# A block difference in expert 0's output: taken from the weights instead of from the result

## The chip, the cores and the metric

The kernel runs on one core of a Trainium2 chip. The metric is the device time of one execution in microseconds; the time before is the median of 13 executions, 684.53 us (684.03 to 687.27). The engines are TensorE (PE in the profile; PEld is its weight load), VectorE (DVE), ScalarE (ACT), GpSimd (POOL) and SyncE (SP), which here only issues DMAs. Each engine works through its own instruction list in the order in which it was written down; semaphores make one engine wait for another.

## The reference

Two layers follow each other. An attention with a narrow band and block summaries takes q, k, v of 4 batches, 8 heads, 768 positions and 64 features, and gives x, 3072 tokens by 512 features. Then a mixture of 8 experts works on x:

```python
logits = x @ w_gate
logits = logits - logits.max()
P = np.exp(logits)
for _ in range(8):                      # Sinkhorn: rows, then columns
    P /= P.sum(1, keepdims=True) + 1e-09
    P /= P.sum(0, keepdims=True) + 1e-09
    P *= N / E
out = np.zeros((N, D), dtype=np.float32)
for e in range(E):
    h = np.maximum(x @ w1[e], 0.0)      # 3072 x 1024
    ye = h @ w2[e]                      # 3072 x 512
    out += P[:, e:e + 1] * ye
```

Every token passes through every expert, so the two matrix products of eight experts are most of the work.

## The kernel before

**Attention and expert 0 (up to about 175 us of the trace).** The attention goes by pairs of heads, four pairs to a batch. Expert 0 is computed beside it in the plain way, because it can begin as soon as a batch's x is there: tokens go in halves of a batch (384 tokens, function `expert0`, called with `t0` = 0, 384, ... 2688). A half has eight hidden blocks (`hidden0`, matmuls at L199, relu on ACT or DVE) and three output tiles of 128 tokens (`project0`, matmuls at L204 that read `w2s[0]`); a tile goes to `out_acc[:, t, :]` with a copy (L195). In `out_acc` it stands unscaled, since the weights P are not known yet.

The order of this stage is not written out by hand. `add(...)` gives a planner (`Plan`) units of work with an engine, a cost in microseconds, the units that they depend on and a priority; the planner simulates the engines and issues the units in the order that comes out. Units of expert 0's matmuls have low priority (1000 and up) and fill gaps; their evacuations have -1.0, which goes ahead of the attention's own units (0 to 35). PSUM tiles are rings of a few buffers ("m" has three, "a" three, "s" one). After the attention, `bridge` adds the Sinkhorn rounds (DVE, POOL and PE in turn) and the first groups of expert 1 to the same plan, and the rest of expert 0's matmuls fill in between.

**Experts 1 to 7 (from about 175 us on).** Here both products are done by a seven-product (Strassen-Winograd) scheme on blocks of halves: tokens t and t + 1536 are taken together. The hand-written loop over `n` computes in each round one hidden group (`group`: four 128-row weight blocks times 512 token pairs, products `p1` to `p7`) and one output pair (`pair`: tile `ta` of the first 1536 tokens and tile `tb` of the second, products `q1` to `q7`). A round has the order `q1 p1 ... q5 v5 ... p6 c2 ... p2 r11 q6 v6 p3 c12 p7 c22 r12 q2 q4 q3 r22 s1 s3 p4 s2 q7`, with names in `p` and `q` on PE, `r12 r22 s1 s2 s3 s4 c12 c22 v5 ya yb` on DVE and the rest on ACT. Into DVE's list between `s4` and `c12` some rounds put sums of weights or of x for the next expert (`w2_sum`, `w1_sums`, `x_sum`). The lines to know: L817 writes `hf<-pb,c` (`c12`), `hf<-pg,c` (`c22`) and `xy<-xy,c` (`v5`); L928 is `r12`, L931 is `r22`, both a relu in place on 128x512 fp16; L1010 is `ya`/`yb`.

The seven-product scheme gives for tile `tb` not the two column halves of the output but the second half and the difference second minus first. So `out_acc[:, tb, 0:DH]` holds, through experts 1 to 7, the difference; `fin` turns it back after expert 7. What expert 0 left there has to be brought into that form. This is done in `scale0`, once for each of the 12 pairs of expert 1, at the end of rounds n = 4 to 15: ACT multiplies both tiles by P[:, 0] (L965), and then GpSimd (L967) replaces the first half columns by second minus first.

POOL's list holds, besides, the loads of the next expert's weights (L175 for w1, L186 for w2), which it issues as DMAs.

Of the kernel before, what the change touches and what calls it, by code (L numbers as in the profile page):

```python
# [13 lines left out]
ALU = mybir.AluOpType  # L14
# [19 lines left out]
class Plan:  # L34
# [12 lines left out]
    def add(self, eng, cost, fn, deps=(), prio=0.0, opens=(), uses=(), lag=0.0):  # L47
        u = Unit(eng, cost, fn, [d for d in deps if d is not None], prio, list(opens), lag)
        for b in list(opens) + list(uses):
            b.users.append(u)  # L50
        if uses and eng != "PE":
            u.prio -= 100.0
        self.waiting.append(u)
        return u
# [62 lines left out]
def kernel(  # L117
# [10 lines left out]
    nc = tc.nc  # L128

    B, H, S, D = q.shape  # L130
    G = S // 128
    N, DM = out.shape
# [3 lines left out]
    KF = F // 128  # L136
# [8 lines left out]
    HG = G // 2  # L145
# [19 lines left out]
    out_acc = persist.tile([128, NT, DM], FP32)  # L165
# [3 lines left out]
    w1s, w2s = {}, {}  # L169
# [27 lines left out]
    def hidden_mm(e, hp, t0, n, f):  # L197
        for dk in range(KD):
            nc.tensor.matmul(hp[:, 0:n], lhsT=w1s[e][:, dk, 128 * f:128 * (f + 1)],  # L199
                             rhs=xT[:, dk, t0:t0 + n], start=(dk == 0), stop=(dk == KD - 1))  # L200

    def project_mm(e, yp, h, c, fs):
        for f in fs:
# [17 lines left out]
    if True:  # L221
# [16 lines left out]
        add = plan.add  # L238
# [291 lines left out]
        def project0(key, c, part):  # L530
            if part == 0:
                at["yp", key, c] = bank("m", "yps")
            project_mm(0, at["yp", key, c], at["h", key], c, range(4 * part, 4 * part + 4))
# [62 lines left out]
        U = {}  # L596
# [114 lines left out]
        def expert0(t0, xs):  # L711
            key, n = t0, len(halves)
            halves.append(key)
            pr = 1000.0 + n
            w = [U["w1", i] for i in range(2)]
            evac, old = [], [U.get(("pj", halves[n - 2], c)) for c in range(HG)] if n >= 2 else []
            for f in range(KF):
                buf = Buffer("m")

                def fn(f=f):  # L720
                    at["hp", key, f] = hidden0(key, t0, f)
                m = U["hd", key, f] = add("PE", 0.67, fn, xs + [w[f // 4]] + old, pr + f * 0.01, opens=[buf])

                def ev(f=f):
                    relu(U["rl", key, f].on, at["h", key][:, f, 0:HS], at.pop(("hp", key, f))[:, 0:HS])
                U["rl", key, f] = add({"ACT": 0.5, "DVE": 0.56}, 0, ev, [m], -1.0, uses=[buf])
                evac.append(U["rl", key, f])
                zero.extend([m, evac[-1]])
            for c in range(HG):
                buf = Buffer("m")  # L730
                p0 = add("PE", 0.88, lambda c=c: project0(key, c, 0), evac[0:4] + [U["w2"]],
                         pr + 0.1 + c * 0.02, opens=[buf])
                p1 = add("PE", 0.88, lambda c=c: project0(key, c, 1), evac[4:8] + [p0],
                         pr + 0.11 + c * 0.02, uses=[buf])
                U["pj", key, c] = p1

                def ev(c=c):
                    copy(U["yo", key, c].on, out_acc[:, t0 // 128 + c, :], at.pop(("yp", key, c))[:])
                U["yo", key, c] = add({"ACT": 0.58, "DVE": 0.68}, 0, ev, [p1], -1.0, uses=[buf])
                zero.extend([p0, p1, U["yo", key, c]])  # L740

        def gate(b, xs, prio):
            buf = Buffer("a")
            U["lg", b] = add("PE", 0.65, lambda: logits(b), xs, prio, opens=[buf])
            U["lo", b] = add("ACT", 0.25, lambda: logits_out(b), [U["lg", b]], prio, uses=[buf])
# [27 lines left out]
        for i in range(PB, NP):  # L773
            load_pair(i)
            pair_start(i, 20 + i)
            pair_whole(i, 20 + i)
            if i % PB == PB - 1:
                b = i // PB
                xs = [U["x", PB * b + d] for d in range(PB)]
                gate(b, xs, 900 if b < B - 1 else 0)  # L780
                expert0(b * S, xs)
                expert0(b * S + HS, xs)
        for i in range(4):
# [15 lines left out]
    if True:  # L799
# [148 lines left out]
        def pair(e, j, c, spare=False, c1_at=None):  # L948
            def h(q):
                return lambda f: hs[e, j, f][:, q, :]  # L950
            ta, tb = 4 * j + c, HT + 4 * j + c
            B = {}

            def part(*ks):
                if not spare:
                    return B["x"][:, ks[0]:ks[-1] + 1:max(1, ks[-1] - ks[0]), :]
                t, k = B["xy"[ks[0] // 2]], ks[0] % 2
                return t[:].rearrange("p (k d) -> p k d", k=2)[:, k:k + 1, :]

            def at(k):  # L960
                return part(k)[:, 0, :]

            def scale0():
                for t in (ta, tb):
                    nc.scalar.activation(out=out_acc[:, t, :], in_=out_acc[:, t, :], func=AF.Copy,  # L965
                                         scale=P_sb[:, t, 0:1])
                nc.gpsimd.tensor_tensor(out=out_acc[:, tb, 0:DH], in0=out_acc[:, tb, DH:DM],  # L967
                                        in1=out_acc[:, tb, 0:DH], op=ALU.subtract)

            def q1():  # L970
                if spare:
                    B["x"] = fps.tile([128, 512], FP32, tag="ab", name="px", bufs=2)
                    B["y"] = fps.tile([128, 512], FP32, tag="g", name="py", bufs=2)
                else:
                    B["x"] = xps.tile([128, 4, DH], FP32, tag="xy", name="xy", bufs=2)
                product2(e, c, at(0), h(A11), "B11", True)

            def c1():
                B["c1"] = c1_at if c1_at is not None else fast.tile([128, DH], FP32, tag="c1", name="c1", bufs=1)[:]
                nc.scalar.copy(out=B["c1"], in_=at(0))  # L980

            def q5():
                product2(e, c, at(1), h(S1), "T1", False)

            def v5():
                plus(at(2), at(1), B["c1"])

            def q6():
                product2(e, c, at(2), h(S2), "T2", False)

            def v6():
                nc.scalar.copy(out=at(3), in_=at(2))

            def q2():
                product2(e, c, at(0), h(A12), "B21", False)

            def q7():
                product2(e, c, at(2), h(S3), "T3", False)

            def q3():  # L1000
                product2(e, c, at(3), h(S4), "B22", False)

            def q4():
                product2(e, c, at(1), h(A22), "T4", False)

            def add(t, k, *src):
                src = part(*src)
                w = src.shape[1]
                acc = out_acc[:, t, k * DH:(k + w) * DH].rearrange("p (h d) -> p h d", h=w)
                nc.vector.scalar_tensor_tensor(out=acc, in0=src, scalar=P_sb[:, t, e:e + 1], in1=acc,  # L1010
                                               op0=ALU.mult, op1=ALU.add)

            def store(t, k=slice(0, DM)):
                nc.sync.dma_start(out=out[t * 128:(t + 1) * 128, k], in_=out_acc[:, t, k])

            def ya():
                add(ta, 0, 0, 3)
                if e == E - 1:
                    store(ta)

            def yb():
                add(tb, 0, 1, 2)

            def fin():
                if e == E - 1:
                    sub(out_acc[:, tb, 0:DH], out_acc[:, tb, DH:DM], out_acc[:, tb, 0:DH])
                    store(tb)

            def y_half():
                add(ta, 1, 3)  # L1030
                add(tb, 1, 2)
                store(tb, slice(DH, DM))
                sub(out_acc[:, tb, 0:DH], out_acc[:, tb, 0:DH], out_acc[:, tb, DH:DM])
                nc.vector.tensor_scalar_mul(out=P_sb[:, tb, 0:1], in0=P_sb[:, tb, e:e + 1], scalar1=-1.0)

            def x_half():
                add(ta, 0, 0)
                store(ta)
                nc.vector.scalar_tensor_tensor(
                    out=out_acc[:, tb, 0:DH], in0=at(1), scalar=P_sb[:, tb, 0:1],  # L1040
                    in1=out_acc[:, tb, 0:DH], op0=ALU.mult, op1=ALU.subtract)
                store(tb, slice(0, DH))

            return {f.__name__: f for f in (scale0, q1, c1, q5, v5, q6, v6, q2, q7, q3, q4, ya, yb, fin, y_half, x_half)}
# [204 lines left out]
```

## Time and profile before

The profiled execution took 684.53 us; its span on the core was 682.8 us, the other 1.7 us lie around it.

| | value |
|---|---|
| median of 13 executions | 684.53 us |
| profiled execution, time / span | 684.53 / 682.8 us |
| DVE busy | 589.5 us (86%) |
| ACT busy | 407.3 us (60%) |
| POOL busy | 134.7 us (20%) |
| POOL's subtraction L967 | 12 times, 719 to 832 ns, first at 178.2, last at 248.9 us |
| matmuls of expert 0, L199 and L204 | 256 and 192 |
| granted TensorE clock | 0.999 |

Reading it: busy time is an average over stages. The trace gives every instruction's start and duration, so a stage with a loop can be judged by the time from one round to the next, and the engine that holds it up by who waits for whom. The ends of matmuls are modelled (several in a row overlap in the listing), so on PE starts are compared with starts.

### The profile page before, as it was taken

The page shows a single profiled execution, that of the slowest core. Times are in us where ns is not written, and L with a number is a line of the kernel's source. Part 1 is how long each engine was busy: PE and PEld are TensorE (multiplying, and loading weights), DVE is VectorE, ACT ScalarE, POOL GpSimd, SP SyncE. Part 2 cuts the span into 40 slices and gives each one's busy share as a digit, 9 for nine tenths or more (in the row PEclk, how much of TensorE's full clock was granted, in tenths as well). Part 3 has the DMA queues.
Part 4 walks back from the last instruction along what each step waited for, and adds up shares of the span by engine and source line. Part 5 has one row for each costly group of instructions (what it writes and reads, how often), then busy time and mean ns, then how long its engine had stood idle before and what let it go on. Part 6 is the DMA issues. An engine that isn't in the chain of part 4 may idle for free.

```text
span 682.8 us, 13662 instructions
## 1 busy us (share of the span) xinstructions
PE 669.0 (98%) x5189; PEld 439.0 (64%) x5189; DVE 589.5 (86%) x1444; ACT 407.3 (60%) x785; POOL 134.7 (20%) x177
## 2 busy tenths in 40 slices
PE   8999999899999999999999999999999999999996
PEld 4666666555666666666666666666666666666665
DVE  6878988777799998999789988998899888998886
ACT  4777877555677765555555555555555555555551
POOL 8699810122213120100101010201010101000000
PEclk9999999999999999999999999999999999999999
DMA  9999990000504023310513050404131051301224
GB/s 117 189 145 144 124 115 7 1 1 0 70 9 47 2 31 48 30 18 1 78 17 32 1 78 1 48 1 60 19 31 17 8 71 17 32 1 48 78 93 155
DMA packets 113618, 33.90 MB, mean 50 GB/s; under 512 B 99984, under 2 KB 110736, under 8 KB 113552
## 3 DMA queue, kind: packets, MB, share of 16 engines
q0 software_dynamic: 104672, 26.22, 42.0%
q1 hardware_dynamic: 8352, 6.80, 3.3%
q8 instruction: 40, 0.66, 0.4%
q14 instruction: 26, 0.21, 0.1%
q10 hardware_dynamic: 528, 0.02, 0.0%
HBM read 52.45 MB, written 6.29 MB: 86 GB/s over the span
## 4 chain that ended last, share of the span: by engine, by line
PE 82%; DVE 12%; issue 2%; DMA 1%; POOL 1%; ACT 1%; DVEq 0%; ACTq 0%
PE xy L873 31%; PE pg L867 14%; PE pb L867 9%; PE pa L867 9%; PE yps L204 6%; PE hps L199 6%; DVE hf L817 3%; DVE out_acc L1010 2%; PE tkq L299 1%; PE sg L318 1%; DVE hf L814 1%; DVE hf L928 1%; DVE xy L817 1%; DMA vx<-in_v_dram 1%; PE vs L326 1%
## 5 line engine op out<-in xcount | busy, mean ns | idle before, releaser
L873 PEld LDWEIGHTS <-hf 128*128 128x128 f16 x2352 | 230.0, 98 | 100.3 <-issue 7.0
L873 PE MATMUL xy<-w,hf 128*128 128x256 f16 x1312 | 183.4, 273 | 0.0
L873 PE MATMUL xy<-ws,hf 128*128 128x256 f16 x984 | 147.6, 272 | 2.3 <-DVE xy L817 1.9
L190 ACT ACTIVATE hf<-pg 128x512 f16<-128x512 f32 x84 | 50.2, 597 | 152.8 <-PE pg L867 152.8
L1010 DVE SCALAR_TENSOR_TENSOR out_acc<-xy,P_sb,out_acc 128x512 f32<-128x512 f32 x164 | 115.0, 742 | 1.3 <-PE xy L873 1.3
L814 DVE TENSOR_TENSOR hf<-hf 128x512 f16<-128x512 f16 x252 | 98.9, 420 | 8.5
L867 PE MATMUL pa<-xT,w 128*128 128x512 f16 x336 | 99.9, 379 | 0.0
L867 PEld LDWEIGHTS <-w 128*128 128x128 f16 x672 | 65.7, 98 | 44.5 <-issue 0.5
L817 DVE TENSOR_TENSOR hf<-pb,c 128x512 f16<-128x512 f32 x84 | 57.9, 690 | 35.6 <-PE pb L867 33.9
L175 POOL DMA_DIRECT2D w<-in_moe_w_dram x56 | 41.9, 759 | 185.3 <-PE pg L867 156.9
L867 PEld LDWEIGHTS <-ws 128*128 128x128 f16 x504 | 49.3, 98 | 24.9
L901 ACT COPY c<-pg 128x512 f32<-128x512 f32 x84 | 49.2, 586 | 22.4 <-PE pg L867 22.4
L817 DVE TENSOR_TENSOR hf<-pg,c 128x512 f16<-128x512 f32 x84 | 57.0, 679 | 0.1
L190 ACT ACTIVATE hf<-pa 128x512 f16<-128x512 f32 x84 | 50.6, 602 | 1.1 <-PE pa L867 1.1
L886 ACT COPY pg<-pa 128x512 f32<-128x512 f32 x84 | 47.9, 570 | 4.7
L867 PE MATMUL pg<-xTs,w 128*128 128x512 f16 x168 | 50.0, 379 | 0.2
L867 PE MATMUL pg<-xT,w 128*128 128x512 f16 x168 | 50.0, 379 | 0.0
L867 PE MATMUL pb<-xTs,ws 128*128 128x512 f16 x168 | 50.0, 379 | 0.0
L867 PE MATMUL pb<-xT,ws 128*128 128x512 f16 x168 | 50.0, 379 | 0.0
L867 PE MATMUL pg<-xTs,ws 128*128 128x512 f16 x168 | 50.0, 379 | 0.0
L894 ACT COPY c<-pb 128x512 f32<-128x512 f32 x84 | 49.7, 592 | 0.0
L199 PE MATMUL hps<-xT,w 128*128 128x384 f16 x256 | 48.9, 326 | 0.0
(136 smaller groups left out, 847.9 us busy)
## 6 DMA issues: line engine op xcount, KB each, us to landing
w<-in_moe_w_dram POOLq DMA_DIRECT2D x8, 1024.0 KB, 9.5
w<-in_moe_w_dram POOLq DMA_DIRECT2D x56, 128.0 KB, 3.6
out_dram<-out_acc SPq DMA_DIRECT2D x22, 256.0 KB, 2.0
qst<-in_q_dram POOLq DMA_DIRECT2D x32, 96.0 KB, 5.9
vx<-in_v_dram POOLq DMA_DIRECT2D x16, 192.0 KB, 6.5
kst<-in_k_dram POOLq DMA_DIRECT2D x24, 96.0 KB, 6.1
w<-in_moe_w_dram POOLq DMA_DIRECT2D x2, 512.0 KB, 8.3
kst<-in_k_dram POOLq DMA_DIRECT2D x4, 192.0 KB, 5.2
```

Of the source, the lines that this page charges most:

```text
L175: nc.gpsimd.dma_start(out=t[:, :, h, :], in_=moe_w1[e].rearrange("(dk p) f -> p dk f", p=128)[:, :, f:f + 128])
L190: nc.scalar.activation(out=out, in_=in_, func=AF.Relu, bias=0.0, scale=1.0)
L199: nc.tensor.matmul(hp[:, 0:n], lhsT=w1s[e][:, dk, 128 * f:128 * (f + 1)], rhs=xT[:, dk, t0:t0 + n], start=(dk == 0), stop=(dk == KD - 1))
L204: nc.tensor.matmul(yp[:], lhsT=h[:, f, c * 128:(c + 1) * 128], rhs=w2s[e][:, f, :], start=(f == 0), stop=(f == KF - 1))
L814: nc.vector.tensor_tensor(out=out, in0=in0, in1=in1, op=ALU.subtract)
L817: nc.vector.tensor_tensor(out=out, in0=in0, in1=in1, op=ALU.add)
L867: nc.tensor.matmul(bank[:], lhsT=w[:, dk, :], rhs=x[:, dk, :], start=start and dk == 0, stop=dk == KH - 1, skip_group_check=True)
L873: nc.tensor.matmul(bank, lhsT=a(f)[:, 128 * c:128 * (c + 1)], rhs=w[:, f, :], start=start and f == 0, stop=f == FH - 1, skip_group_check=True)
L886: nc.scalar.copy(out=B["g"][:], in_=B["a"][:])
L894: nc.scalar.copy(out=B["c5"][:], in_=B["b"][:])
L901: nc.scalar.copy(out=B["c2"][:], in_=B["g"][:])
L1010: nc.vector.scalar_tensor_tensor(out=acc, in0=src, scalar=P_sb[:, t, e:e + 1], in1=acc, op0=ALU.mult, op1=ALU.add)
```

## The change

Expert 0's projection for the second 1536 tokens uses, in the first half columns, w2[:, second half] - w2[:, first half], which gives the difference directly: (h @ B) - (h @ A) = h @ (B - A). `w2_difference` writes it over the first half columns of `w2s[0]`, in four DVE instructions of 128x(2x256) fp16. They depend on all twelve output tiles of the first 1536 tokens (which still need the old columns), and every projection of the second 1536 tokens depends on them. They have priority -1.0. The subtraction on GpSimd is taken out of `scale0`.

```diff
+    def w2_difference(f):
+        f = slice(f, f + KF // 4)
+        nc.vector.tensor_tensor(out=w2s[0][:, f, 0:DM // 2], in0=w2s[0][:, f, DM // 2:DM],
+                                in1=w2s[0][:, f, 0:DM // 2], op=ALU.subtract)
...
-                p0 = add("PE", 0.88, lambda c=c: project0(key, c, 0), evac[0:4] + [U["w2"]],
+                p0 = add("PE", 0.88, lambda c=c: project0(key, c, 0), evac[0:4] + (U["w2d"] if t0 >= N // 2 else [U["w2"]]),
                          pr + 0.1 + c * 0.02, opens=[buf])
...
                 gate(b, xs, 900 if b < B - 1 else 0)
+                if b == B // 2:
+                    done = [U["pj", t, c] for t in halves for c in range(HG)]
+                    U["w2d"] = [add("DVE", 0.33, lambda f=f: w2_difference(f), done, -1.0)
+                                for f in range(0, KF, KF // 4)]
+                    zero.extend(U["w2d"])
                 expert0(b * S, xs)
                 expert0(b * S + HS, xs)
...
                     nc.scalar.activation(out=out_acc[:, t, :], in_=out_acc[:, t, :], func=AF.Copy,
                                          scale=P_sb[:, t, 0:1])
-                nc.gpsimd.tensor_tensor(out=out_acc[:, tb, 0:DH], in0=out_acc[:, tb, DH:DM],
-                                        in1=out_acc[:, tb, 0:DH], op=ALU.subtract)
```

## The prediction

> **What bounds the kernel now.** I read the page's busy times first, then the distance from round to round in the listing of PE by time, then one round on all engines, then the stretch of the attention in which the new instructions will stand.
>
> ```profile
> PE 669.0 (98%) x5189; PEld 439.0 (64%) x5189; DVE 589.5 (86%) x1444; ACT 407.3 (60%) x785; POOL 134.7 (20%) x177
> ```
>
> PE is busy for 98% of the span, so a change can only win where PE loses time. The list of who waits for whom puts few waits on PE after 175 us, but busy times and waits are rough here because the ends of matmuls are modelled. The starts of one instruction per round, the product p3, are exact:
>
> ```profile
> 182.75 0.59 PE L867 MATMUL pb<-xT,ws 128*128 128x512 f16 x2
> ...
> 247.00 0.59 PE L867 MATMUL pb<-xT,ws 128*128 128x512 f16 x2
> 253.43 0.59 PE L867 MATMUL pb<-xT,ws 128*128 128x512 f16 x2
> 259.50 0.59 PE L867 MATMUL pb<-xT,ws 128*128 128x512 f16 x2
> ```
>
> From 253.43 to 259.50 is 6.07 us; the rounds from 260.21 to 320.99 (starts of c12 in DVE's listing) take 60.78 / 10 = **6.078** us each, with PE back to back. From 182.75 to 253.43 eleven rounds take 70.68 us, **6.43** each: 0.35 us per round more for the same matmuls. The round before (176.12 to 182.75) took 6.63. These are the twelve rounds with the GpSimd subtraction. One of them, all engines:
>
> ```profile
> 202.73 0.69 DVE L817 TENSOR_TENSOR hf<-pb,c 128x512 f16<-128x512 f32 x1 [0.26 <-PE pb L867]
> 203.34 0.68 DVE L817 TENSOR_TENSOR hf<-pg,c 128x512 f16<-128x512 f32 x1
> ...
> 203.91 0.73 POOL L967 TENSOR_TENSOR out_acc<-out_acc 128x256 f32<-128x256 f32 x1 [5.70 <-ACT out_acc L965]
> 203.94 0.85 DVE L928 TENSOR_SCALAR hf<-hf 128x512 f16<-128x512 f16 x1
> ...
> 204.71 0.28 DVE L931 TENSOR_SCALAR hf<-hf 128x512 f16<-128x512 f16 x1
> ...
> 207.24 0.59 PE L867 MATMUL pa<-xT,w 128*128 128x512 f16 x2
> ...
> 207.55 0.42 DVE L817 TENSOR_TENSOR xy<-xy,c 128x256 f32<-128x256 f32 x1
> ...
> 208.03 0.60 PE L873 MATMUL xy<-ws,hf 128*128 128x256 f16 x4 [0.19 <-DVE xy L817]
> ...
> 209.16 0.69 DVE L817 TENSOR_TENSOR hf<-pb,c 128x512 f16<-128x512 f32 x1 [0.26 <-PE pb L867]
> ```
>
> The columns are start, duration, engine, line, operation; the bracket is idle time before it and who ended it. DVE does c12 and c22, then POOL's subtraction starts at 203.91, and r12, which starts 0.03 us later, takes 0.85 us. Further down, PE begins `pa` at 207.24; two matmuls take it to 207.67 (starts 0.43 apart), but its next product q6 starts at 208.03, 0.06 after v5 ended on DVE (207.55 + 0.42 = 207.97). So 0.36 us of PE is lost to DVE once a round. The same place in a round without POOL:
>
> ```profile
> 297.28 0.68 DVE L817 TENSOR_TENSOR hf<-pg,c 128x512 f16<-128x512 f32 x1
> ...
> 297.88 0.28 DVE L928 TENSOR_SCALAR hf<-hf 128x512 f16<-128x512 f16 x1
> ...
> 298.08 0.28 DVE L931 TENSOR_SCALAR hf<-hf 128x512 f16<-128x512 f16 x1
> ```
>
> There r12 takes 0.28 us. The stage is held by a DVE list made 0.57 us longer (0.85 - 0.28) by POOL; everything after r12 comes later by that.
>
> **The removed subtraction.** Twelve of them, 0.73 us each on POOL, which is 20% busy: their own time is worth nothing. Their worth is what they do to DVE. The chain that closes in a round is c12 to v5 on DVE (202.73 to 207.97, 5.24 us), v5 to q6 to p3 on PE and to the next c12 (207.97 to 209.16, 1.19). Sum 6.43, the measured round. With r12 at 0.28 it is 6.43 - 0.57 = 5.86, below the 6.08 that PE needs. So PE is next, with 0.22 to spare, and a round gains 0.35, not 0.57. DVE's total work does not hold it either: 6.43 less 0.26 idle less 0.57 is 5.60 per round, and 5.86 in the rounds with four 0.28 us weight sums in place of one sum of 0.68. ACT keeps its two scalings (1.34 us); in the round shown it then idled 1.00 us for PE before the next relu, so it is not late.
> Sum over the stage: eleven rounds, 70.68 - 11 x 6.078 = 3.82. The first round gains 0.27: its 6.63 becomes 6.08 + 0.28, because p4 waits there for a c22 that follows four sums of w2, with or without POOL. Together 4.1. Against it: in the round at 228.80, c12 starts 0.29 us after its engine fell free, for no reason that I find in the trace; I let that remain and take off 0.25. **3.85 us.**
>
> In POOL's list the weight loads at 178.87 to 181.31 stood behind the first subtraction at 178.20. They can now go as soon as their buffers are free, up to some 5 us earlier. Expert 2's w2 is first summed at 201.79, so nothing waits for them and no store runs then: 0.
>
> Here the Trainium skill is to be weighed. "SBUF — State Buffer", section "Who interferes with whom", calls the DVE/GpSimd port pair an exclusive lock: the second to come is blocked until the first has finished. By that, r12 would lose 0.70 us (203.94 to 204.64) and the twelve rounds 8.4; by the row it is 0.57, and 6.8. Both exceed PE's 0.35, so the sum is the same by either; that the later instruction pays is what matters.
>
> **The added subtractions.** Four DVE tensor_tensor, 512 fp16 elements per partition each, both inputs in SBUF. The nearest row has the same size and type:
>
> ```profile
> L814 DVE TENSOR_TENSOR hf<-hf x252: 361/418/747, 140.9 to 666.3; 128x512 f16<-128x512 f16 x126
> ```
>
> Median 0.418, so 4 x 0.42 = **1.67** us of DVE. Bounds: 0.38 each where such instructions follow each other (two took 0.76 at 205.55), 0.75 each if they met something on POOL; POOL is idle from 100 to 125 us, so I take 0.42. This stretch of the trace is where the built program puts them:
>
> ```profile
> 109.36 1.04 PE L204 MATMUL yps<-w,h 128*128 128x512 f16 x4
> ...
> 110.20 0.48 DVE L337 COPY Ve<-Ve 64x650 bf16<-64x650 bf16 x1
> ...
> 110.61 0.54 DVE L367 TENSOR_TENSOR em<-er,band 128x768 bf16<-128x768 bf16 x1
> ...
> 112.26 0.55 DVE L367 TENSOR_TENSOR em<-er,band 128x768 bf16<-128x768 bf16 x1
> ```
>
> The twelfth tile of the first half ends with the projection at 109.36 (to 110.40); DVE is free of the copy at 110.68. The instruction order of the changed program has on DVE: two differences, relu, difference, relu, difference, relu, then both mask products `em` (before: 110.61 and 112.26), then the four edge instructions. With the rows' durations and the relus not before their matmuls (the first at 111.78), the last difference ends at 113.75 and the second `em` at 115.4, where it was 112.81; the edges end at 116.3, where it was 114.83. Who waits for that:
>
> ```profile
> 114.85 0.35 PE L390 MATMUL av<-vx,em 128*128 128x65 bf16 x6
> ...
> 119.07 2.75 PE L204 MATMUL yps<-w,h 128*128 128x512 f16 x12
> ```
>
> The attention's values (114.85) need the edges. The planner has put a score product (0.31 us from start to start) and two hidden blocks (0.65 each) ahead of them on PE: work that was to come later anyway, 1.6 us, to 116.5. So 1.6 us of lateness is covered by 1.6 of work. If the cover fails, PE stands for the difference: 0 to 1.5 us. The relus of hidden blocks that wait behind the differences free "m" buffers: that of the third hidden block ends at 114.3, and the PE product that needs its buffer comes at about 115.2. The new wait (projections of the second 1536 tokens for the differences) is met with ease: such a projection first stands on PE at 119.07, in the new order at about 119.3, 5.5 us after 113.75. From the next-but-one projection on PE's order is as before; gate and Sinkhorn begin where they did (DVE idled 3.27 us before the Sinkhorn's first reduction at 126.97). DVE was busy only 2.48 of the 5 us from 120 to 125, where the lateness is worked off. Below zero: a reordered plan can also close one of the small gaps here; PE shows no more than some 0.5 us of them. Bounds -0.4 to +1.5, taken **+0.2**, near the lower end since the cover was worked out row by row.
>
> A rule speaks against the change: "Perfetto Trace Analysis", "Optimizing Scalar/DVE Operations", says that when DVE is saturated, moving work from it to GpSimd may make sense. DVE is 86% busy, and this moves work the other way. By that rule alone the change costs 1.67 us and the result is 686.2. The same section adds that the two share a port and that moving work between them might not help; this trace puts a number on it: each GpSimd subtraction took 0.57 us of DVE, 6.8 in all, four times what replaces them, and at the place where DVE is late.
>
> **Sum.** -3.85 + 0.2 = -3.65: span 679.15, time 684.53 - 3.65 = **680.9**. The profiled execution took exactly the median, so nothing is corrected between them. About 0.2%, 1.4 us, is what a measurement of this kernel can tell from no change.
>
> **Rivals.**
> 1. Another wait comes in at about half the gain. For it: the spare 0.22 us between 5.86 and 6.08 is small, and DVE had no idle time at all in the rounds with four weight sums. Against: the rounds at 290.60 to 308.83 have the same sums, no idle either, and take 6.08. At 6.25 a round: 12 x 0.18 = 2.2, less 0.2: 682.5. Chance 0.11.
> 2. No gain: r12 only absorbs time that DVE would wait anyhow. For it: DVE idles 0.26 before each c12. Against: that wait is for p3, which follows the q6 that DVE itself delayed. Time 684.7. Chance 0.05.
> 3. Slower: the planner's new order starves PE in the attention. The place is the values behind the late `em` at 116.5, and the "m" ring, whose relus now stand behind the differences. It decides once PE loses over 5.3 us there, that is 3.85 plus the 1.4 of the bound; it would take the differences at over twice their row, and the lateness carried through a second pair. At 6 us lost: 686.7. Chance 0.05.
> That the change does not do what it says is no case here: the POOL list of the changed program has no subtraction of `out_acc` left and DVE's has the four differences.
>
> **Numbers.** Forecast 0.79 at 680.9, own range 680.2 to 681.9; with rival 1 the range is 680.0 to 682.7. Faster by over 0.2%: 0.79 + 0.11 less a little for its slow end, 0.88; within: 0.07; slower: 0.05.
>
> **What would show it.** r12 at 0.28 in all rounds; p3 to p3 at 6.08 from 183 us on; no wait of PE for v5; four L204 differences on DVE at about 110.7 to 113.8, 0.42 each; and PE's gate and first Sinkhorn product within 1 us of 125.95 and 129.44. Wrong if rounds stay at 6.25 or more, or if the gate comes over 1.5 us late.

## The result, and the profile after

The changed kernel takes **680.47 us** (median of 11 executions, 679.21 to 683.62) against 684.63 for the kernel before (48 executions); the ratio is 0.9931, 95% interval 0.9916 to 0.9947. Faster, as forecast, by more: on the 684.53 us of the prediction the ratio gives 679.8 (678.8 to 680.9), 0.4 below the low end of the forecast's own range (680.2) and 0.2 below that of the wider range with rival 1 (680.0); the forecast of 680.9 is the upper end of the interval. The profiled execution took 679.21 us, its span is 677.5 (684.53 and 682.8 before).

The page of the changed kernel, busy times of the engines:

```profile
PE 666.4 (98%) x5189; PEld 438.9 (65%) x5189; DVE 585.3 (86%) x1447; ACT 406.9 (60%) x786; POOL 125.7 (19%) x165
```

PE is at 98% as before: the span shrank with its idle time. The listing of PE by time, the product p3 once a round:

```profile
181.52 0.59 PE L877 MATMUL pb<-xT,ws 128*128 128x512 f16 x2
...
242.30 0.59 PE L877 MATMUL pb<-xT,ws 128*128 128x512 f16 x2
...
248.38 0.59 PE L877 MATMUL pb<-xT,ws 128*128 128x512 f16 x2
```

From 181.52 to 248.38 eleven rounds take 66.86 us, 6.08 each, where they took 70.68. One round on DVE and PE, from c12 to the q6 of the next pair:

```profile
194.38 0.69 DVE L827 TENSOR_TENSOR hf<-pb,c 128x512 f16<-128x512 f32 x1 [0.38 <-PE pb L877]
...
195.58 0.28 DVE L938 TENSOR_SCALAR hf<-hf 128x512 f16<-128x512 f16 x1
...
195.78 0.28 DVE L941 TENSOR_SCALAR hf<-hf 128x512 f16<-128x512 f16 x1
...
198.72 0.43 DVE L827 TENSOR_TENSOR xy<-xy,c 128x256 f32<-128x256 f32 x1
198.89 0.59 PE L877 MATMUL pa<-xT,w 128*128 128x512 f16 x2
...
199.32 0.60 PE L883 MATMUL xy<-ws,hf 128*128 128x256 f16 x4
...
200.46 0.69 DVE L827 TENSOR_TENSOR hf<-pb,c 128x512 f16<-128x512 f32 x1 [0.37 <-PE pb L877]
```

r12 (now L938) takes 0.28 us. v5 starts at 198.72, ahead of `pa`, so that q6 follows `pa` after 0.43 us (198.89 to 199.32): no time of PE is lost to DVE. Before c12 DVE waits 0.37 us for PE, where it was 0.26. The attention, where the four differences (L204) stand:

```profile
109.66 0.74 DVE L204 TENSOR_TENSOR w<-w 128x512 f16<-128x512 f16 x2
...
111.31 0.41 DVE L204 TENSOR_TENSOR w<-w 128x512 f16<-128x512 f16 x1
...
112.30 0.41 DVE L204 TENSOR_TENSOR w<-w 128x512 f16<-128x512 f16 x1
...
113.09 1.02 DVE L372 TENSOR_TENSOR em<-er,band 128x768 bf16<-128x768 bf16 x2
...
114.31 1.47 PE L199 MATMUL hps<-xT,w 128*128 128x384 f16 x8
...
115.63 0.35 PE L395 MATMUL av<-vx,em 128*128 128x65 bf16 x6
```

They take 0.41 us each, from 109.66 to 112.71; both `em` end at 114.11, and the values on PE start at 115.63, right behind the two hidden blocks from 114.31.

Where the 5.32 us between the two profiled spans lie, by starts of the same instruction in both:

| stretch | before | after | difference |
|---|---|---|---|
| start to the gate of the first batch | 39.34 | 38.40 | -0.94 |
| first gate to the gate of the last batch (holds the differences) | 86.61 | 86.60 | -0.01 |
| last gate to p3 of round 4 (Sinkhorn, rest of expert 0) | 50.17 | 50.18 | +0.01 |
| p3 of round 4 to p3 of round 16 (the twelve rounds) | 77.31 | 73.20 | -4.11 |
| p3 of round 16 to p3 of round 83 | 407.96 | 407.46 | -0.50 |
| from there to the end | 21.43 | 21.66 | +0.23 |

The first line lies ahead of the change, and over the twelve profiled executions of this study the first gate came anywhere from 38.40 to 40.45, whatever the kernel: I take it as scatter. The rounds hold the gain. The 0.50 behind them and the 0.23 of the last line had no place in the forecast. The last line is no scatter: it is a pause of DVE ahead of one write of `py`, a tile of the last rounds, here in the kernel before and then in the changed one:

```profile
668.71 0.43 DVE L817 TENSOR_TENSOR py<-px,c 128x256 f32<-128x256 f32 x1 [1.16 <-PE px L873]
```

```profile
663.51 0.43 DVE L827 TENSOR_TENSOR py<-px,c 128x256 f32<-128x256 f32 x1 [1.51 <-PE py L883]
```

The idle time is 0.35 us longer, and PE is 0.23 later from its next product on. Experiments 7 and 8 show where such pauses come from.

### The profile page after: what moved, and what is told of

It reads as the page before. It is cut to its first block, busy times and chain, and to the rows that moved or that the text cites. A ratio compares the mean times of both kernels' runs of the same rounds, so it can differ in the third digit from the quotient of the medians.

```text
span 677.5 us, 13654 instructions
## 1 busy us (share of the span) xinstructions
PE 666.4 (98%) x5189; PEld 438.9 (65%) x5189; DVE 585.3 (86%) x1447; ACT 406.9 (60%) x786; POOL 125.7 (19%) x165
## 4 chain that ended last, share of the span: by engine, by line
PE 91%; DVE 5%; issue 1%; DMA 1%; POOL 1%; ACT 0%; DVEq 0%; ACTq 0%
PE xy L883 36%; PE pg L877 16%; PE pb L877 10%; PE pa L877 10%; PE yps L209 6%; PE hps L199 6%; PE tkq L304 1%; PE sg L323 1%; DVE out_acc L1018 1%; PE vs L331 1%; PE tx L506 1%; DMA qst<-in_q_dram 1%; PE av L395 1%; PE av L401 1%; PE av L468 0%
```

## The experiments

**1. The removal alone.**

```diff
-                nc.gpsimd.tensor_tensor(out=out_acc[:, tb, 0:DH], in0=out_acc[:, tb, DH:DM],
-                                        in1=out_acc[:, tb, 0:DH], op=ALU.subtract)
```

> The kernel before without the GpSimd subtraction, and nothing put in its place: the first half columns of the second 1536 tokens keep expert 0's plain result, so the output differs there. Theory (the subtraction costs what it blocks of DVE, the rest of the change costs nothing): rounds at 6.08 us in place of 6.43, p3 of the first round to p3 twelve rounds later 73.2 us in place of 77.3, time 4.1 us below the kernel before and the same as the changed kernel within 0.5. Rival (part of the changed kernel's gain lies in its new order of the attention): rounds as fast, but 0.5 to 1 us slower than the changed kernel in total.

680.63 us, ratio 0.9938 (0.9921 to 0.9955): the whole gain, as far as the two intervals can tell. First gate to last gate 86.60, so the new order in the attention is worth nothing, and the rival falls. Rounds of 6.08, but the twelve took 73.68 us and not 73.2: round 4 (6.58) and round 12 (6.31) were longer by 0.24 each. In DVE's listing of this kernel, v5 of the round after the first:

```profile
181.14 0.43 DVE L817 TENSOR_TENSOR xy<-xy,c 128x256 f32<-128x256 f32 x1 [0.23 <-PE pg L867]
```

It idles 0.23 us ahead of it, and the releaser named, PE's `pg`, is not what v5 needs: in the same round of the changed kernel v5 starts at 180.53 while `pg` (from 180.22) is still running. This is the pause at 228.80 of the prediction met again at another place; experiments 5 to 8 are about it.

**2. The addition alone.** The changed kernel with the two removed lines back in `scale0`, so that the difference is taken twice.

> The changed kernel with the GpSimd subtraction put back behind the scaling, so that the difference is taken twice and the output differs in those columns: it has the added part of the change alone. Theory (the four differences on DVE are covered in the attention): the time of the kernel before within 0.5 us, rounds at 6.43 again, gate of the last batch as far from the first gate as before (86.6 us). Rival (the new order gives or takes something by itself): more than 0.7 us away from the kernel before while its rounds are at 6.43.

684.26 us, ratio 0.9991 (0.9974 to 1.0009). First gate to last gate 86.60, the twelve rounds 77.35. The four differences cost nothing that can be measured, and the rounds' gain comes from the removal.

**3. The subtraction at another moment.**

```diff
-                for t in (ta, tb):
+                for t in (tb, ta):
```

> The kernel before with the two scalings in scale0 exchanged: tile tb first, so that the subtraction starts about 0.67 us earlier, beside c22 (one input in PSUM, one in SBUF) and not beside r12. Theory (a shared port: only what needs the second port is held up): r12 at 0.28 to 0.33 us, c22 unchanged at 0.68, rounds at 6.08 to 6.12, time 3.6 to 4.1 us below the kernel before, with the subtraction still there. Rival (GpSimd at work slows whatever DVE does then): c22 takes 1.0 us or more and the rounds stay at 6.3 to 6.43.

A round of this kernel, DVE and POOL:

```profile
203.41 0.68 DVE L817 TENSOR_TENSOR hf<-pg,c 128x512 f16<-128x512 f32 x1
203.56 0.73 POOL L967 TENSOR_TENSOR out_acc<-out_acc 128x256 f32<-128x256 f32 x1 [5.35 <-ACT out_acc L965]
...
204.01 0.44 DVE L928 TENSOR_SCALAR hf<-hf 128x512 f16<-128x512 f16 x1
...
204.37 0.28 DVE L931 TENSOR_SCALAR hf<-hf 128x512 f16<-128x512 f16 x1
```

The subtraction now starts beside c22, which takes its 0.68 us all the same; r12 gets 0.44 and not the 0.28 to 0.33 expected, because POOL started at 203.56 and not 203.25. The rounds are at 6.08, the twelve of them 73.73 us (round 12 with a pause, as in experiment 1): all but 0.05 of what the removal alone gives (73.68), with all twelve subtractions still there. The time is 682.04 us, ratio 0.9954 (0.9936 to 0.9972), somewhat less gain than the rounds promise, though its interval overlaps that of experiment 1. So GpSimd's work did not slow c22, but it did stop r12. In this round r12 ended at 204.45, 0.16 after POOL's 204.29; in the round of the prediction at 204.79, 0.15 after POOL's 204.64. The two overlaps with POOL are 0.28 and 0.70 us long, and r12 ends at the same distance behind POOL: it behaves as if let through only when the subtraction is done, with 0.12 of its 0.28 us spent by then. The order of the two decides who waits: in one round of the kernel before, r12 starts at 236.08, 0.04 ahead of POOL, and takes its usual 0.28; POOL takes 0.83 and not 0.73 there, and r22, which comes next, takes 0.82.

**4. The subtraction on DVE**, ahead of `ya` in the next round:

```diff
             def ya():
+                if e == 1:
+                    sub(out_acc[:, tb, 0:DH], out_acc[:, tb, DH:DM], out_acc[:, tb, 0:DH])
                 add(ta, 0, 0, 3)
```

> The kernel before with the twelve subtractions moved from GpSimd to DVE, ahead of ya in the next round. Theory (a round is the longer of PE's 6.08 and the chain through DVE, 5.86 without the block): the chain gets 0.42 us, 6.28 us a round, so 12 x 0.15 = 1.8 us below the kernel before and 2.4 above the changed one. Rival (the 0.22 us of spare time that was read off the trace is larger, so that PE stays the bound): rounds at 6.08 to 6.12 and the time of the changed kernel within 0.5 us.

The rounds took 6.20 us (eleven in 68.18): neither 6.28 nor 6.08. In its listing:

```profile
209.83 0.76 DVE L814 TENSOR_TENSOR hf<-hf 128x512 f16<-128x512 f16 x2
...
210.51 0.42 DVE L814 TENSOR_TENSOR out_acc<-out_acc 128x256 f32<-128x256 f32 x1
...
210.84 1.40 DVE L1008 SCALAR_TENSOR_TENSOR out_acc<-xy,P_sb,out_acc 128x512 f32<-128x512 f32 x2
...
213.77 0.69 DVE L817 TENSOR_TENSOR hf<-pb,c 128x512 f16<-128x512 f32 x1
```

The subtraction is listed with 0.42 us, but the next instruction starts 0.33 after it (210.51 to 210.84). The chain is 5.86 + 0.33 = 6.19, near the measured 6.20. So the 5.86 of the prediction is right, the 0.22 us to spare too, and this DVE instruction in a row cost its start-to-start time, not the listed one. Time 681.0 us, ratio 0.9946 (0.9926 to 0.9965).

**5 and 6. The pauses: lists made longer.** Tiny memsets among DVE's first constants; four in the kernel before, eight in the changed one.

```diff
             nc.vector.memset(warm, 0.0)
+            for _ in range(4):
+                nc.vector.memset(warm, 0.0)
```

> The kernel before with four tiny DVE memsets (one partition, 8 elements) more among its first constants: DVE's instruction list is four longer, as in the changed kernel, and nothing else differs. Theory (single rounds of 6.3 us come from a pause of DVE at fixed places of its instruction list, and a shift of the list moves the places): the pattern of the changed kernel, one long round at n = 59 in place of three at 27, 51 and 75, p3 of round 16 to p3 of round 83 in 407.46 us in place of 407.96. Rival (the change itself removes them, by way of its weights or its queues): the pattern of the kernel before, 407.96.

> The changed kernel with eight such memsets more, so that its DVE list is twelve longer than before, as it was with the subtraction on DVE. Theory (places in the list): no long round at all after n = 16, 407.25 us from round 16 to 83. Rival (chance from execution to execution): long rounds at 59 or elsewhere.

Both expectations failed. These two kernels and those of experiments 7, 8 and 9 were executed once each, so only their traces are compared, not their times. With four more in the kernel before: long rounds at 20, 35, 44, 59 and 68, 408.40 us. With eight more in the changed kernel: 27, 51, 59 and 75, 408.12 us. So the places move with the length of the list, but I had counted wrongly. Entries of DVE's list in the built programs, with the waits that stand as entries of their own: 1752 before, 1755 after (four differences more and one entry less, a piece of work of the attention stage that the new plan gives to ACT), 1756 in experiment 5.

**7 and 8. The pauses: the count put right.** Three memsets in the kernel before, one in the changed kernel.

> The kernel before with three tiny DVE memsets more among its first constants. Counted with its waits, the DVE list is 1752 entries in the kernel before, 1755 in the changed one and 1756 in the two kernels with long rounds at 20, 35, 44, 59 and 68; so three, not four, put the entries of experts 1 to 7 where the changed kernel has them. Theory (DVE pauses at every 64th entry of its list, and PE loses where such an entry is v5 or close before it): long rounds as in the changed kernel, 59 alone, 407.46 us from round 16 to 83, with the subtraction still there (rounds of 6.43 before). Rival (something else of the change): 407.96 with 27, 51 and 75, or another pattern.

> The changed kernel with one tiny DVE memset more, 1756 entries. Theory (every 64th entry): long rounds at 20, 35, 44, 59 and 68, 408.4 to 408.6 us from round 16 to 83, 1 us more than the changed kernel. Rival: 407.46 with 59 alone.

The second came as expected: 20, 35, 44, 59 and 68, 408.61 us. The first had no long round at all, 407.25 us: 27, 51 and 75 went, but 59 was not there. The lists tell more. In the kernels before and in experiments 1 and 3, v5 of the rounds after 27, 51 and 75 is entry 832, 1216 and 1600 of DVE's list: 13, 19 and 25 times 64; the paused v5 of experiment 1 is entry 448, 7 times 64; the paused c12 at 228.80 is entry 576, 9 times 64. In experiment 5, and in 8 with the same count, v5 after rounds 35 and 59 is entry 960 and 1344, and the entry 11 ahead of v5, which is c12, is a multiple of 64 in the other three (704, 1088, 1472); in experiment 6 it is c12 of rounds 27, 51 and 75 (832, 1216, 1600).

All these numbers are odd multiples of 64, and the traces show that only those count. A c12 or v5 that stands right behind a wait in the list starts 0.04 to 0.09 us after that wait has ended. In all twelve traces, from p3 of round 16 to p3 of round 83, 27 of them are odd multiples of 64, and every one starts 0.39 to 0.41 us after its wait; 24 are even multiples, and none is late; of 1557 at other numbers none is late either. So the pause comes once in 128 entries, as far as it can be seen. Where such a number falls on an instruction that follows another without a wait, no idle time shows. The `py` of the last rounds is entry 1728, 27 times 64, in the three kernels whose list is three entries longer (the changed kernel, experiments 2 and 7), and these three alone need 21.66 or 21.67 us at the end in place of 21.4 to 21.5.

Round 59 in the changed kernel has another source: ACT's list is one entry longer there too, and the copy c2 of that round is entry 832 of ACT's list, where it was 831. ACT of the changed kernel in that round, and v5 on DVE of the kernel before after round 27:

```profile
503.06 0.59 ACT L911 COPY c<-pg 128x512 f32<-128x512 f32 x1 [0.28 <-PE pg L877]
...
509.41 0.59 ACT L911 COPY c<-pg 128x512 f32<-128x512 f32 x1 [0.56 <-PE pg L877]
```

```profile
325.69 0.43 DVE L817 TENSOR_TENSOR xy<-xy,c 128x256 f32<-128x256 f32 x1 [0.36 <-PE pg L867]
```

ACT idles 0.56 us ahead of c2, where it idles 0.28 in the round before. v5 idles 0.36 where the rounds around it have none. Kernels with the ACT list of the kernel before (experiments 1, 3, 4, 5 and 7) show no such idle time of ACT there; the others, with the changed list (2, 6, 8, 9 and 10), all show the same 0.56 at c2; where this meets DVE's pause (experiments 8 and 10) round 59 takes 6.53 us and not 6.3. On ACT the rule is less clear: the copies at entries 832 and 960 are late, the relu at 704 is not. That places are set by the program and repeat from kernel to kernel is shown; what happens at these entries (the loading of instructions is a guess) is not.

**9. Twice the differences.** Each followed by a second one of the same size into a scratch tile.

```diff
+        nc.vector.tensor_tensor(out=spare2[:], in0=w2s[0][:, f, DM // 2:DM],
+                                in1=w2s[0][:, f, 0:DM // 2], op=ALU.subtract)
```

> The changed kernel with each of the four differences followed by a second DVE subtraction of the same size into a scratch tile: 1.65 us more of DVE at the same place, the order otherwise the same. Theory (the cover in the attention is used up by the four): the third hidden block's relu and the edges end 1.65 us later, PE stands 0.8 to 1.6 us, first gate to last gate 87.4 to 88.2 us in place of 86.6. Rival (DVE has more to spare there than was read): 86.6 to 87.0.

First gate to last gate 87.42 us, 0.82 more than with four, at the lower edge of what was expected. The stretch where it is lost:

```profile
115.07 0.55 DVE L193 TENSOR_SCALAR h<-hps 128x384 f16<-128x384 f32 x1
...
115.67 1.46 PE L200 MATMUL hps<-xT,w 128*128 128x384 f16 x8
...
117.20 0.20 DVE L387 TENSOR_TENSOR Ee<-er,band 32x80 bf16<-32x80 bf16 x1
...
117.23 0.52 PE L404 MATMUL av<-Ve,Ee 128*128 128x130 bf16 x3
```

The first row is the relu of the third hidden block: it ends at 115.62, and only then is its buffer free for the two hidden blocks on PE (115.67). In the changed kernel they begin at 114.31; this trace runs 1.19 us later at the start of the stretch, so they are 0.17 late, and the first values behind them 0.15 (116.97 against 115.63). The last two rows: the values' second part waits for the edges, done at 117.40, so that the next values stand at 117.59 against 115.99, 1.60 apart, 0.26 more. The remaining 0.41 comes between there and the last gate (127.00 against 125.00); its cause is open. `em` itself, done at 116.56, was still not what PE waited for. Of 1.65 us more on DVE 0.83 were covered: the cover in the attention was about that much deeper than the forecast used, and rival 3 of the prediction, a loss of over 5.3 us, was out of reach even with twice the differences. What broke the cover first were the buffer of the third hidden block and the edges, the two places that the prediction had named.

**10. A try at a faster version.** The changed kernel with the planner's lag of the column sums raised.

```diff
-step = add(eng, us, fn, [step], -50.0, opens=o, uses=w, lag=(0.9 if n else 2.0) if fn is columns else 0.0)
+step = add(eng, us, fn, [step], -50.0, opens=o, uses=w, lag={0: 3.0, 1: 2.0}.get(n, 0.9) if fn is columns else 0.0)
```

> The changed kernel with the planner told that the column sums of the first two Sinkhorn rounds are ready later (lag 3.0 and 2.0 us in place of 2.0 and 0.9), which puts PE's two small products of these rounds behind more of expert 0's matmuls. Theory (PE waits 0.78 and 0.93 us for these sums): last gate to p3 of round 4 in 48.5 us in place of 50.2, time 1.5 to 1.7 us below the changed kernel, 5.5 to 6 below the kernel before. Rival (the wait comes back at a later Sinkhorn round or in the order around it): 49.5 to 50.2 us and no measurable gain.

Last gate to p3 of round 4 took 49.63 us, 0.55 less, not 1.7: PE no longer waits for the two sums, but for 0.81 us at 136.97 for the x sums on DVE, which the new order puts later. Its DVE list has 1756 entries, so the 67 later rounds took 408.62, 1.16 more. Time 683.2 us, ratio 0.9967 (0.9952 to 0.9983); in 8 of its 15 executions the granted clock was 0.991 to 0.994, and its ratio includes these. The other seven have a median of 680.39 us, which can't be told from the changed kernel's 680.47. None of the ten experiments shows a gain over the changed kernel.

## Why the prediction was right and where it was off

The mechanism of the gain was right; the size was not. The sum was -3.65 us, and the traces show -4.38: three terms were each set on the side of less gain, as the list says in order.

- *DVE is held by POOL's subtraction, 0.57 us a round.* Right: gone with the subtraction (experiment 1), there with it (experiment 2), down to 0.16 when the subtraction starts beside another instruction (experiment 3).
- *PE is next at 6.08, with 0.22 us to spare.* Right: 6.08, and the chain of 5.86 showed itself when 0.33 was added (experiment 4). Rival 1, half the gain at 6.25 a round, and rival 2, no gain, fall with it.
- *3.82 and 0.27 for the rounds, less 0.25 for the pause at 228.80.* The first two make 4.09; measured 4.11. **The 0.25 taken off is the first term that failed**: the pause belongs to entry 576 of DVE's list, and the list shifted, so that nothing of it was left. With the list unshifted (experiment 1) pauses do remain, 0.48 us of them, and the rounds give 3.63.
- *The added differences: 1.67 us of DVE, covered, +0.2 on PE.* Measured 1.65 and -0.01. **The +0.2 is the second.** The working of what PE does until the values was right (the values were forecast for 116.5, and stand at 116.58 when 0.95 is added for the earlier gate of this trace); I took a remainder for safety that the trace did not ask for. Experiment 9 shows how much more was covered.
- *Nothing behind round 16.* **The third, put at nothing: it is -0.27.** Three pauses of 0.24 us turned into one of 0.21, through the length of two instruction lists (-0.50), and one came in at the end (+0.23). The kernel before with nothing but three tiny instructions more (experiment 7) has the same end of 21.67 and no pause in the rounds. The long rounds could be seen in the trace of before; the prediction took them as fixed.
- Sum of what the traces show: -4.11 - 0.01 + 0.01 - 0.50 + 0.23 = -4.38, or 680.15 us on 684.53. The three terms together are 0.73 us (0.26, 0.20 and 0.27). The ratio says 679.8, another 0.35 less; that lies inside its interval (678.8 to 680.9), and no run here assigns it to a cause.
- *The lock by the Trainium skill ("SBUF — State Buffer", section "Who interferes with whom"), 0.70, or by the row, 0.57.* Experiment 3 reconciles them: the blocked instruction ends 0.15 to 0.16 us after the other, so it is blocked to the end, as the page has it, but with about 0.12 of its own time spent before. Its loss is so much less than the overlap.
- *The rule on a saturated DVE.* Read the other way round, as the prediction did, it speaks against the change. Experiment 4 is the move to DVE in its plainest form, 12 x 0.33 us more on the engine that is 86% busy, and it gains over the kernel before; it is still behind the four differences, 74.78 against 73.20 us for the twelve rounds.

## What to carry to other kernels

Look for an instruction that is far longer in one stage than in another, and at what runs on GpSimd then: the price of a GpSimd instruction can be what it holds up; here its start 0.4 us earlier beside c22 was worth as much in the rounds as its removal. In a loop, compare the chain through the second engine with the bound of the first before counting a gain: here 0.57 us were freed and 0.35 gained. A forecast to within half a microsecond on 680 has to count small pauses too, which here came and went with edits that changed the length of an instruction list.

## What was not expected of the hardware

- DVE pauses once in 128 entries of its list, at the odd multiples of 64: a c12 or v5 there, right behind a wait, starts 0.39 to 0.41 us after it in place of 0.04 to 0.09 (27 of 27; at even multiples 0 of 24). It costs PE about 0.24 us when it falls on an instruction in the chain. The same rounds were long in kernels with DVE lists of the same length (27, 51, 75 in three; 20, 35, 44, 59, 68 in three), and the 67 rounds took 407.25 to 408.62 us with these pauses as the only difference found. The cause is open.
- A DVE instruction with one input in PSUM and one in SBUF (c22) kept its 0.68 us beside a GpSimd subtraction, while a relu in fp16 on SBUF that started 0.03 us after the subtraction took 0.85 us in place of 0.28.
- Back to back on DVE, a 128x256 fp32 subtraction listed with 0.42 us takes 0.33 of the engine's time.
